# Pooling attention and a tanh-shrink MLP: four steps around batch 1 and batch 2 put in another order

## The chip, the cores and the metric

The kernel runs on one core of one Trainium2 chip. The metric is the device time of one execution in microseconds, and for several executions their median. Each time is that of a whole launch; the profile shows one execution on the same core, with a span a little shorter than the time measured around it.

## What is computed

Eight batches of eight heads, 576 positions, head size 64. Keys and values are averaged over groups of eight positions, so that each head has 72 pooled keys. Attention follows, and its output goes through an MLP whose activation is h - tanh(h).

```python
k_p = k.reshape(B, H, Sp, pool, D).mean(axis=3)
v_p = v.reshape(B, H, Sp, pool, D).mean(axis=3)
scores = scale * np.matmul(q, k_p.transpose(0, 1, 3, 2))
attn = softmax(scores)                     # over the 72 pooled keys
x = np.matmul(attn, v_p).transpose(0, 2, 1, 3).reshape(B * S, H * D)
h = x @ w_in                               # 4608 x 512 @ 512 x 2048
out = (h - np.tanh(h)) @ w_out             # @ 2048 x 512
```

## The kernel before, in words

The schedule is written out by hand. Each engine runs its instructions in the order of the text, and an instruction that waits holds up all behind it on its engine. The 4608 rows are cut in nine groups of 512. Group g < 8 is the first 512 positions of batch g; group 8 gathers the last 64 positions of all batches.

**Group 0** multiplies plainly: L588 makes h (mlp_h_mms), L599 and L601 the tanh and the difference, L616 (mlp_o) the product with w_out, in four quarters `qd` of four blocks `tb`. Between these matmuls stands the attention of batch 1: its keys are turned on TensorE (k_transpose, L352) and copied by VectorE to KB (L342, L343, L346); its q, which GpSimd's software queue has loaded as bf16 into the space of w2s[4], is reordered into q_bf (L1017, one half by VectorE, the other by ScalarE), turned on TensorE (q_pe_transpose, L228, evacuated by ScalarE at L144; q_pe_tail, L240), and used for the scores (L398). VectorE pools the values (pool_v1, L303 and L323). The product of attention and values is L487; VectorE divides it by the sum (L522, L523) into x_sb; TensorE turns x_sb (turn1, L566) and ScalarE copies it to xT (L573).

**Groups 1 to 8** use a product with seven block products in place of eight. For it, sums of blocks of w_out must be made: sum0 to sum3, `negated` and w_sum, all by w_sum at L674 (VectorE, for sum3 GpSimd) except `negated` (ScalarE, L996). They stand among the instructions of group 0 and the first pairs of group 1. Four of GpSimd's sums are released by `placed`, the last instruction of pool_v1(2, 4). In each group seven pairs of hidden tiles (h_pair, L634 on TensorE, L647 tanh on ScalarE, L648 difference on VectorE) are followed by the block products (L691); between these stand the scores (head_scores, L446, banks in pairs 2,3 then 4,5 then 0,1) and the attention output (L472) of the next batch. The banks of the pairs in group 1 are (6, 4, 2, 6, 0, 2, 4).

**q and k of batch 2 on** go through DMA transposes issued by SyncE (SP): k_dma_transpose at L374, q_dma_transpose at L214 and L219, after ScalarE's casts q_cast_part at L196 and L201. In group 1 the cast and the transpose of part p - 3 stand ahead of pair p, for p = 3, 4, 5. On SP the DMA issues are in order as well: the stores of group 0 (L707), the transpose of x (L557), the transpose of the keys of batch 2, which waits for GpSimd's pooling (L270), then the loads of batch 3. The loads of w_in and w_out (L761, L768), of v of batch 0 (L831) and q of batch 1 (L841, L842) are issued by GpSimd, behind its memsets.

PSUM banks are handed out in turn by ps_any; for batch 1 it draws on banks 4 to 7.

Of the kernel before, what the change touches and what calls it, by code (L numbers as in the profile page):

```python
# [43 lines left out]
def kernel(  # L44
# [9 lines left out]
    nc = tc.nc  # L54
# [43 lines left out]
    w2s = const.tile([128, 5, NP, HD], F16, name="w2s")  # L98
# [50 lines left out]
    def load_main(src, dst, b, t0, t1, eng=nc.sync):  # L149
        return eng.dma_start(out=dst[:, t0:t1, :], in_=src[b, 0:128, t0:t1, :])  # L150
# [12 lines left out]
    def load_k(b, eng=nc.sync):  # L163
        return [
            load_main(k_pairs, k_raw[b % 2], b, 0, NM, eng),
            load_dense(k_pairs, k_raw[b % 2], b, eng),
        ]
# [25 lines left out]
    def q_cast_part(b, n):  # L193
        t = q_raws[b]
        if n < 2:
            nc.scalar.copy(  # L196
                out=q_bf[:, 2 * n : 2 * n + 2, :, :].rearrange("p j h d -> p h j d"),
                in_=t[:, :, 2 * n : 2 * n + 2, :],
            )
        else:  # L200
            nc.scalar.copy(out=q_bf[:QT, R, :, :], in_=q_raws.pop(b)[:QT, :, R, :])  # L201
# [21 lines left out]
    def q_pe_transpose(b, hps, eng=None):  # L223
        qT, _ = q_tiles(b)
        for hp in hps:
            ps = ps_any([128, QA], FP32, "qT_ps")
            for j in range(R):
                nc.tensor.matmul(  # L228
                    ps[:, j * 128 : (j + 1) * 128],
                    lhsT=q_bf[:, j, 2 * hp : 2 * hp + 2, :].rearrange("p h d -> p (h d)"),  # L230
                    rhs=ident[:, :],
                    start=True,
                    stop=True,
                )
            evac(qT[:, :, hp, :], ps.rearrange("p (j c) -> p j c", j=R), eng)
# [64 lines left out]
    def pool_v1(ta, tb):  # L300
        r = v_raw[1].rearrange("p t (j d) -> p t j d", d=D)
        for n in (4, 2, 1):
            nc.vector.tensor_tensor(  # L303
                out=r[:, ta:tb, 0:n, :],
                in0=r[:, ta:tb, 0:n, :],
                in1=r[:, ta:tb, n : 2 * n, :],
                op=ALU.add,
            )
        if ta == NM:
            return v_left(VB[1], r[:, NM, 0:1, :], nc.vector)  # L310
        return v_main(VB[1], r[:, :, 0:1, :], nc.vector, ta, tb)
# [48 lines left out]
    def k_transpose(b, alloc, engs=(nc.vector.tensor_copy, nc.scalar.copy)):  # L360
        kd = kdups.pop(b)
        ps = alloc([128, NM, 128], FP32, "kT_ps")
        for t in range(NM):
            turn_tile(ps[:, t, :], kd, t)
        kb_main(KB[b % 2], ps, 0, NM, engs)
        ps = alloc([128, 128], FP32, "kT_ps")
        turn_tile(ps[:, :], kd, NM)
        kb_left(KB[b % 2], ps, nc.vector.tensor_copy)
# [3 lines left out]
    def k_dma_transpose(b):  # L372
        kT = work.tile([128, NT, 128], BF16, name="kT", tag="kT", bufs=1)
        nc.sync.dma_start_transpose(  # L374
            out=kT[:, :, :], in_=kdups.pop(b)[:, :, :, :].rearrange("p t a d -> p (t a d)")
        )
        kTs[b] = kT
# [232 lines left out]
    def mlp_o(g, tb, qd, gts):  # L610
        if qd == 0:
            o_tiles[tb] = bank((1, 2, 3, 0)[tb], [128, DM])
        o_ps = o_tiles[tb]
        i0 = W2_ORDER[qd]
        for i in range(i0, i0 + 4):
            nc.tensor.matmul(  # L616
                o_ps[:, :],
                lhsT=gts[i][:, tb * 128 : (tb + 1) * 128],
                rhs=w2b[:, i, :],
                start=(i == 0),  # L620
                stop=(i == NHID - 1),
            )
        if qd == 3:
            if tb < 2:
                nc.vector.tensor_copy(out=O[:, tb, :], in_=o_ps[:, :])
            else:
                nc.scalar.copy(out=O[:, tb, :], in_=o_ps[:, :])
            if tb % 2:
                store(g, tb - 1, tb + 1, nc.sync)
# [136 lines left out]
    def load_w2(i, n):  # L766
        w2_dmas.append(
            nc.gpsimd.dma_start(out=w2b[:, i : i + n, :], in_=w2_src[:, i : i + n, :])  # L768
        )
# [39 lines left out]

    make_identity(nc, ident)  # L810
    nc.gpsimd.memset(q_bf[64:128, R, :, :], 0.0)
    nc.gpsimd.memset(w2s[64:128, 3, 6:8, :], 0.0)
    nc.gpsimd.memset(mask[:, :, :], 1.0)
    for m, base, step, cm in (
        (mask[:, 0 : 2 * NM : 2, 0], G - 1, 0, -1),
# [27 lines left out]
        out=q1_bf, in_=q[1, :, 0:QA, :].rearrange("h (p j) d -> p h j d", j=R)  # L843
    )
    load_w2(8, 4)
    nc.gpsimd.memset(k_raw[1][:, NM, :], 0.0)
    nc.gpsimd.memset(v_raw[0][:, NM, :], 0.0)
    nc.gpsimd.memset(KB[1][:, :], 0.0)
# [67 lines left out]
    gts = []  # L916
# [84 lines left out]
    def sum0(k0):  # L1001
        return w_sum(w2s[:, 0, :, :], b11, b22, ALU.add, k0=k0, k1=k0 + 4)

    def sum1(k0):
        return w_sum(w2s[:, 1, :, :], b11, b12, ALU.add, k0=k0, k1=k0 + 4)
# [7 lines left out]
    pool_k(1, nc.gpsimd, last=nc.vector)  # L1013
    load_w2(4, 4)
    load_w2(12, 4)
    for h, copy in ((0, nc.vector.tensor_copy), (4, nc.scalar.copy)):
        copy(  # L1017
            out=q_bf[:, 0:R, h : h + 4, :].rearrange("p j h d -> p h j d"),
            in_=q1_bf[:, h : h + 4, :, :],
        )  # L1020
    mlp_o(0, 0, 0, gts)
    mlp_o(0, 1, 0, gts)
    mlp_o(0, 2, 0, gts)
    k_transpose(1, ps_any, (nc.vector.tensor_copy, nc.vector.tensor_copy))
    mlp_o(0, 3, 0, gts)
    q_pe_transpose(1, (0, 1), "act")
    sum1(0)
    pool_v1(0, 2)
    q_pe_transpose(1, (2, 3), "act")
    q_pe_tail(1)  # L1030
    scores_wide(1, (0,))
    placed = pool_v1(2, 4)
    mlp_o(0, 0, 1, gts)
    scores_wide(1, (1,))
    mlp_o(0, 1, 1, gts)
# [27 lines left out]
    turn1(3)  # L1063
    av(1, 4, ps_any, True)
    sum0(4)
    for tb in range(4):
        mlp_o(0, tb, 3, gts)
    x_pairs.pop((1, 0))
    x_pairs.pop((1, 1))
    x_dma_transpose(1, 2)  # L1070
    pool_k(2, nc.gpsimd)
    k_dma_transpose(2)
    load_k(3)
    pool_v(2, nc.gpsimd, (0, 1))
    k_place(2, nc.gpsimd.tensor_copy)
# [2 lines left out]
    for g in range(1, NG):  # L1078
        nb = g + 1 if g + 1 < B else None
        nn = g + 2 if g + 2 < B else None  # L1080
        for p in range(NP - 1):
            if g == 1 and 3 <= p < 6:
                q_cast_part(2, p - 3)
                q_dma_transpose(2, p - 3)
            if nb is not None and g > 1 and p < 3:
                q_cast_part(nb, p)
            h_pair(g, p, ((6, 4, 2, 6, 0, 2, 4) if g == 1 else (0, 2, 4, 6, 0, 2, 4))[p], p % 2)
            if g == 1 and p == 1:
                sum2(4)
            if g == 1 and p == 2:  # L1090
                w_sum(b12, b22, b12, ALU.subtract)
            if g == 1 and p == 5:
                load_v(3)
                load_q(3)
                v_spread(2, nc.gpsimd)
            if 3 <= p < 6:
                sum_p(2 * p - 6, 2 * p - 4)
            if g > 1 and p == 0:
                if nb is not None:
                    k_dma_transpose(nb)  # L1100
                store(g - 1, 2, 4, nc.gpsimd)
                store(g - 1, 0, 2, nc.gpsimd)
                if nb is not None:
                    k_place(nb, nc.gpsimd.tensor_copy)
            if nb is not None and g > 1 and p < 3:
                q_dma_transpose(nb, p)
            if nb is not None and g > 1 and p == 2:
                v_spread(nb)
                if nn is not None:
                    load_k(nn)  # L1110
                    load_v(nn)
                    load_q(nn)
        h_one(g, NP - 1, 1, 0, 2)
        h_one(g, NP - 1, 0, 1, 3)
        sum_p(6, 8)
        sum_q(0, 4)
        sum_q(4, 8)
        if nb is not None:
            sum_d(0, 2)
            sum_d(2, 4)  # L1120
        ps_a = Banks(2, 3, 4, 5, 0, 1)
        for u in range(14):
            n, half = u // 2, u % 2
            bk, lhs, rhs = products[n]
            if n == 6 and g == NG - 1:
                break
            product(g, bk, lhs, rhs, 4 * half, 4 * half + 4, n < 2)
            if half:
                after_product(g, n)
            if nb is not None:  # L1130
                if u == 0:
                    head_scores(nb, (0, 1))
                if u == 2:
                    head_scores(nb, (2, 3), True)
                if u in (5, 6, 7, 8, 10):
                    blk = (5, 6, 7, 8, 10).index(u)
                    av(nb, blk, ps_b1, True)
                    if blk in (1, 3, 4):
                        x_dma_transpose(nb, blk // 2)
                if u == 6 and nn is not None:  # L1140
                    pool_k(nn, nc.gpsimd)
                    pool_v(nn, nc.gpsimd)
        if g < NG - 1:
            nc.scalar.copy(out=O[:, 0:2, 0:HD], in_=chain(g, C1))  # L1144
# [37 lines left out]
```

## Time and profile before

| what | us |
|---|---|
| median of three runs | 286.86 (286.77 to 288.04) |
| the profiled execution, its own time | 286.49 |
| its span | 284.7 |
| TensorE matmul busy | 275.9 |
| VectorE busy | 224.2 |
| ScalarE busy | 155.5 |
| GpSimd busy | 119.1 |

The busy time is that of the whole span. Below, lines are shown of the chain of work that ended last (start, length, what) and of timelines (start, length, engine, line, operation, tiles and shape, count, and in brackets the idle time of the engine before it with what ended it). Several instructions of one kind in a row are merged into one line with their count. PE is TensorE, DVE VectorE, ACT ScalarE, POOL GpSimd, SP SyncE.

### The profile page before, as it was taken

The page shows a single profiled execution, that of the slowest core. Times are in us where ns is not written, and L with a number is a line of the kernel's source. Part 1 is how long each engine was busy: PE and PEld are TensorE (multiplying, and loading weights), DVE is VectorE, ACT ScalarE, POOL GpSimd, SP SyncE. Part 2 cuts the span into 40 slices and gives each one's busy share as a digit, 9 for nine tenths or more (in the row PEclk, how much of TensorE's full clock was granted, in tenths as well). Part 3 has the DMA queues.
Part 4 walks back from the last instruction along what each step waited for, and adds up shares of the span by engine and source line. Part 5 has one row for each costly group of instructions (what it writes and reads, how often), then busy time and mean ns, then how long its engine had stood idle before and what let it go on. Part 6 is the DMA issues. An engine that isn't in the chain of part 4 may idle for free.

```text
span 284.7 us, 5459 instructions
## 1 busy us (share of the span) xinstructions
PE 275.9 (97%) x2156; PEld 180.2 (63%) x2156; DVE 224.2 (79%) x339; ACT 155.5 (55%) x208; POOL 119.1 (42%) x129
## 2 busy tenths in 40 slices
PE   7899999998999999999999999999999999999994
PEld 2454455644894489448954895479547954884583
DVE  5569898789875998599859985998599839936983
ACT  2837676386628672857186718670868056216610
POOL 8810809972299019901990099009910110010000
PEclk9999999999999999999999999999999999999998
DMA  7999999889847894769789986896640540012014
GB/s 245 230 210 279 259 206 305 270 236 229 246 83 144 290 324 83 143 226 350 130 107 270 324 149 124 272 323 131 114 161 0 76 157 0 2 74 77 0 39 111
DMA packets 66731, 49.82 MB, mean 175 GB/s; under 512 B 42088, under 2 KB 55928, under 8 KB 66706
## 3 DMA queue, kind: packets, MB, share of 16 engines
q1 hardware_dynamic: 56082, 34.92, 48.8%
q0 software_dynamic: 8432, 12.72, 18.8%
q10 hardware_dynamic: 2192, 1.84, 2.2%
q8 instruction: 17, 0.28, 0.5%
q14 instruction: 8, 0.07, 0.1%
HBM read 36.70 MB, written 9.44 MB: 162 GB/s over the span
## 4 chain that ended last, share of the span: by engine, by line
PE 90%; DMA 4%; ACT 2%; issue 1%; DVE 1%; ACTq 0%
PE PS L634 36%; PE PS L691 35%; PE PS L588 5%; PE PS L616 5%; PE PS L472 3%; PE PS L446 3%; DMA qT<-q_bf 2%; DMA q_raw<-in_q_dram 2%; PE PS L398 1%; PE PS L781 1%; PE PS L487 1%; ACT q_bf L196 1%; ACT qT L144 1%; PE PS L875 0%; PE PS L936 0%
## 5 line engine op out<-in xcount | busy, mean ns | idle before, releaser
L634 PE MATMUL PS<-xT,w1b 128*128 128x512 bf16 (+1 forms) x504 | 98.0, 355 | 0.0
L648 DVE TENSOR_TENSOR Gt<-PS,TS 128x1024 bf16<-128x1024 f32 x56 | 68.4, 1222 | 33.7 <-ACT TS L647 33.7
L634 PEld LDWEIGHTS <-w1b 128*128 128x128 f16 x576 | 56.3, 98 | 52.8
L647 ACT ACTIVATE TS<-PS 128x1024 f32<-128x1024 f32 x56 | 57.4, 1025 | 29.5 <-PE PS L634 27.4
L735 POOL TENSOR_TENSOR m<-O,m 128x512 f32<-128x512 f32 x6 | 7.6, 1259 | 77.3 <-ACT m L733 77.3
L691 PE MATMUL PS<-w2s,Dg 128*128 128x256 f16 x256 | 30.2, 273 | 0.0
L467 ACT ACTIVATE E<-PS 72x1024 bf16<-72x1024 f32 (+1 forms) x30 | 26.1, 930 | 4.8 <-PE PS L446 4.6
L691 PEld LDWEIGHTS <-Gt 128*128 128x128 bf16 x256 | 23.6, 98 | 6.9 <-issue 2.5
L261 POOL TENSOR_TENSOR k_raw<-k_raw 128x512 f32<-128x512 f32 (+2 forms) x13 | 21.1, 1636 | 14.6 <-DMA k_raw<-in_k_dram 14.6
L691 PEld LDWEIGHTS <-P 128*128 128x128 bf16 x256 | 24.6, 98 | 3.0
L691 PEld LDWEIGHTS <-Dg 128*128 128x128 bf16 x256 | 24.6, 98 | 2.8
L656 DVE TENSOR_TENSOR P<-Gt 128x1024 bf16<-128x1024 bf16 x32 | 22.0, 687 | 0.5
L707 POOL DMA_DIRECT2D out_dram<-O x14 | 7.7, 551 | 31.7 <-DVE O L745 29.5
L742 ACT COPY m<-PS 128x512 f32<-128x512 f32 x8 | 4.7, 586 | 29.6 <-PE PS L691 29.6
L666 DVE TENSOR_TENSOR Dg<-Gt 128x1024 bf16<-128x1024 bf16 x32 | 20.4, 683 | 0.0
L523 DVE TENSOR_TENSOR x_sb<-PS,rden 128x512 bf16<-128x512 f32 x28 | 19.4, 692 | 1.0
L282 POOL TENSOR_TENSOR v_raw<-v_raw 128x512 f32<-128x512 f32 (+1 forms) x12 | 18.2, 1537 | 0.0
L691 PE MATMUL PS<-w2s,Gt 128*128 128x256 f16 x128 | 16.4, 273 | 0.0
L691 PE MATMUL PS<-w2b,P 128*128 128x256 f16 x128 | 16.3, 273 | 0.0
L691 PE MATMUL PS<-w2s,Q 128*128 128x256 f16 x128 | 16.3, 272 | 0.0
L691 PE MATMUL PS<-w2b,Gt 128*128 128x256 f16 x128 | 16.3, 272 | 0.0
L1144 ACT COPY O<-PS 128x512 f32<-128x512 f32 x7 | 4.1, 587 | 21.9 <-PE PS L691 21.9
(125 smaller groups left out, 403.9 us busy)
## 6 DMA issues: line engine op xcount, KB each, us to landing
k_raw<-in_k_dram SPq DMA_DIRECT2D x7, 1024.0 KB, 5.9
out_dram<-O POOLq DMA_DIRECT2D x14, 512.0 KB, 4.3
v_raw<-in_v_dram SPq DMA_DIRECT2D x6, 1024.0 KB, 8.0
q_raw<-in_q_dram SPq DMA_DIRECT2D x6, 1024.0 KB, 10.6
w1b<-in_moe_w_in_dram POOLq DMA_DIRECT2D x4, 512.0 KB, 13.3
w2b<-in_moe_w_out_dram POOLq DMA_DIRECT2D x4, 512.0 KB, 16.6
v_raw<-in_v_dram SPq DMA_DIRECT2D x2, 512.0 KB, 12.5
out_dram<-O SPq DMA_DIRECT2D x2, 512.0 KB, 3.5
```

The costliest lines, as they stand in the source:

```text
L261: eng.tensor_tensor(out=r[:, ta:tb, 0:4, :], in0=r[:, ta:tb, 0:4, :], in1=r[:, ta:tb, 4:8, :], op=ALU.add,)
L282: eng.tensor_tensor(out=r[:, ta:tb, 0:4, :], in0=r[:, ta:tb, 0:4, :], in1=r[:, ta:tb, 4:8, :], op=ALU.add,)
L467: nc.scalar.activation(out=e, in_=ps, func=ACT.Exp, scale=SCALE)
L523: nc.vector.tensor_tensor(out=x_sb[:, :, :, :], in0=ps[:, :, :, 0:D], in1=rden[:, :, :, :].to_broadcast([128, 2, 4, D]), op=ALU.mult,)
L588: nc.tensor.matmul(h_tiles[i][:, :], lhsT=w1b[:, fb, i * 128 : (i + 1) * 128], rhs=xT[g][:, :, fb, :], start=(fb == 0), stop=(fb == NFB - 1),)
L616: nc.tensor.matmul(o_ps[:, :], lhsT=gts[i][:, tb * 128 : (tb + 1) * 128], rhs=w2b[:, i, :], start=(i == 0), stop=(i == NHID - 1),)
L634: nc.tensor.matmul(dst[:, t0 * 128 : t1 * 128], lhsT=w1b[:, fb, i * 128 : (i + 1) * 128], rhs=x[:, t0:t1, fb, :], start=(fb == 0), stop=(f ...
L647: nc.scalar.activation(out=t2, in_=PS[:, b0 : b0 + 2, :], func=ACT.Tanh)
L648: nc.vector.tensor_sub(out=Gt[:, p, :, :], in0=PS[:, b0 : b0 + 2, :], in1=t2)
L656: nc.vector.tensor_tensor(out=P[:, a:b, :], in0=Gt[:, a:b, 0, :], in1=Gt[:, a:b, 1, :], op=ALU.add)
L666: return nc.vector.tensor_tensor(out=Dg[:, a:b, :, :], in0=Gt[:, a:b, :, 0:HT], in1=Gt[:, a:b, :, HT:TG], op=ALU.subtract,)
L691: nc.tensor.matmul(part(g, bk, tt), lhsT=lhs(k, slice(tt * 128, (tt + 1) * 128)), rhs=rhs[:, k, :], start=(first and k == 0 and (tt == 0 o ...
```

## The change

1. A memset of the last rows of q's tail of batch 1 (GpSimd, L812) moves from ahead of the mask and the first loads to a place behind the load of the third quarter of w_out.
2. The second half of the reordering of q of batch 1 goes from ScalarE to VectorE; the first two pairs of q's turns on TensorE go ahead of mlp_o(0, 3, 0); sum1(0) goes behind pool_v1(2, 4).
3. The stores of group 0, which mlp_o(0, tb, 3) issues, go behind the transposes of x's last rows and of the keys of batch 2 on SP.
4. In group 1 the casts and transposes of q of batch 2 stand one pair sooner, and with them the loads of v and q of batch 3 and the spread of v.

```diff
     make_identity(nc, ident)
     nc.gpsimd.memset(q_bf[64:128, R, :, :], 0.0)
-    nc.gpsimd.memset(w2s[64:128, 3, 6:8, :], 0.0)
     nc.gpsimd.memset(mask[:, :, :], 1.0)
...
     load_w2(8, 4)
+    nc.gpsimd.memset(w2s[64:128, 3, 6:8, :], 0.0)
     nc.gpsimd.memset(k_raw[1][:, NM, :], 0.0)
...
-    for h, copy in ((0, nc.vector.tensor_copy), (4, nc.scalar.copy)):
-        copy(
+    for h in (0, 4):
+        nc.vector.tensor_copy(
             out=q_bf[:, 0:R, h : h + 4, :].rearrange("p j h d -> p h j d"),
             in_=q1_bf[:, h : h + 4, :, :],
         )
...
     k_transpose(1, ps_any, (nc.vector.tensor_copy, nc.vector.tensor_copy))
+    q_pe_transpose(1, (0, 1), "act")
     mlp_o(0, 3, 0, gts)
-    q_pe_transpose(1, (0, 1), "act")
-    sum1(0)
     pool_v1(0, 2)
     q_pe_transpose(1, (2, 3), "act")
     q_pe_tail(1)
     scores_wide(1, (0,))
     placed = pool_v1(2, 4)
+    sum1(0)
     mlp_o(0, 0, 1, gts)
...
-    for tb in range(4):
-        mlp_o(0, tb, 3, gts)
     x_pairs.pop((1, 0))
     x_pairs.pop((1, 1))
     x_dma_transpose(1, 2)
     pool_k(2, nc.gpsimd)
     k_dma_transpose(2)
+    for tb in range(4):
+        mlp_o(0, tb, 3, gts)
     load_k(3)
...
-            if g == 1 and 3 <= p < 6:
-                q_cast_part(2, p - 3)
-                q_dma_transpose(2, p - 3)
+            if g == 1 and 2 <= p < 5:
+                q_cast_part(2, p - 2)
+                q_dma_transpose(2, p - 2)
...
-            if g == 1 and p == 5:
+            if g == 1 and p == 4:
                 load_v(3)
                 load_q(3)
                 v_spread(2, nc.gpsimd)
```

## The prediction

> **What bounds the kernel now.** I read the page first, then the chain of work that ended last, then the timelines of the engines around the edited lines.
>
> ```profile
> PE 275.9 (97%) x2156; PEld 180.2 (63%) x2156; DVE 224.2 (79%) x339; ACT 155.5 (55%) x208; POOL 119.1 (42%) x129
> ```
>
> TensorE is busy 97% of the span, and the chain is 90% PE. The change removes no matmul, so only the holes in PE's stream can be won. From 20 us on, the busy time by stage has three stretches with holes: 0.21 us between 30 and 40 us, 0.15 between 40 and 50, 0.85 between 60 and 70. Every other stretch up to 270 us is full. The chain shows two of the three places.
>
> ```profile
> 37.21 0.86 PE PS L616 x4
> 38.07 0.24 PE PS L228 x4
> 38.31 0.02 issue
> 38.33 0.25 ACT qT L144
> 38.58 0.21 issue
> 38.82 0.60 ACT qT L144
> 39.42 0.04 issue
> 39.46 0.38 PE PS L398
> ...
> 63.51 6.34 DMA qT<-q_bf
> 69.84 0.14 issue
> 69.98 0.62 PE PS L446 x4
> ```
>
> At 38 us PE turns q of batch 1 and waits for ScalarE to empty the banks (L144). Near 70 us it waits for the second DMA transpose of q of batch 2, which started when its ScalarE cast ended at 63.48.
>
> The next lines are the VectorE timeline, then the GpSimd timeline (start, duration, engine, line).
>
> ```profile
> 43.13 1.64 DVE L674 TENSOR_TENSOR w2s<-w2b 128x1024 f16<-128x1024 f16 x1
> 45.21 0.69 DVE L523 TENSOR_TENSOR x_sb<-PS,rden 128x512 bf16<-128x512 f32 x1
> 81.06 1.93 DVE L743 TENSOR_TENSOR m<-m,m 128x512 f32<-128x512 f32 x1 [0.46 <-ACT m L742]
> ```
>
> ```profile
> 42.70 1.53 POOL L674 TENSOR_TENSOR w2s<-w2b 128x512 f16<-128x512 f16 x1 [7.24 <-DVE VB L323]
> 44.19 1.59 POOL L674 TENSOR_TENSOR w2s<-w2b 128x512 f16<-128x512 f16 x1
> 80.91 1.54 POOL L267 TENSOR_TENSOR k_raw<-k_raw 128x640 f32<-128x640 f32 x1
> ```
>
> A weight sum on VectorE costs 0.69 us alone (sum1(0) at 38.22), but the one at 43.13 took 1.64 and ended at 44.77, which is 0.58 after GpSimd's operation ended at 44.19. L743 shows the same: shortest 0.69, here 1.93, ended 0.54 after GpSimd's add at 82.45. So a VectorE add with two SBUF inputs that finds GpSimd in an operation waits for its end, then runs some 0.58 more. GpSimd waits in turn: its 1.53 and 1.59 are 1.15 in the two of that group that met no VectorE sum.
>
> **What the Trainium skill says.** "SBUF — State Buffer", section "Who interferes with whom": a VectorE instruction with two SBUF inputs and a GpSimd instruction that reads SBUF share one port; the second to issue blocks wholly until the first is done. The trace agrees (1.64 against 0.69, 1.93 against 0.69). "DMA: Bandwidth & Descriptors", section "Issuing engines are not separate DMA queues": transfers of all issuers run on the same 16 DMA engines and interleave. The trace agrees for the loads after 9 us; before 8.4 us the software queue has no packet at all, though its first issue began at 4.36.
>
> **Part A, the memset.** It occupies GpSimd from 1.91 to 2.43; without it the software-queue issues that follow (v at 4.36, w1 from 5.92, w2 at 8.86) come about 0.5 us sooner. The later ones (q of batch 1 at 11.13, w2 at 12.78) sit behind a cast that waits until 10.58 for another load, so they do not move. At its new place it delays three memsets by 0.5; GpSimd is idle there for 14.37 us until 29.47, and the dense k load that needs one of them is issued at 18.87. Packets of the software queue now begin between 8.4 and 8.6; 0.5 sooner they meet only the tail of the first loads, since the q piece on the chain had landed at 7.30 and the k piece by 8.13. Upper bound: half the engines taken for 0.5 us, +0.25. Lower bound: the queue, full until q of batch 1 lands at 36.5, drains sooner, but VectorE is busy with kd until 36.44, so its q copy at 36.60 gains at most 0.13. I take 0.
>
> **Part B, q of batch 1.** ScalarE's copy cost 1.05 (36.60 to 37.65), VectorE's 0.43. With both on VectorE, q is complete at about 37.40. PE now turns the first two head pairs directly after the keys at 37.21, which need only the first half (ready 37.03), and the 0.86 us of L616 lie behind them while ScalarE empties the banks. Before, PE took 39.46 - 37.21 = 2.25 for this piece; its work is 0.86 + 16 turns at 0.055 (0.88) + 0.12 for the tail = 1.86. Gain 0.39: the scores start at 39.07. I find no new wait in it: the banks of the other two pairs are emptied by VectorE's key copies at about 38.4, and PE comes at 38.51.
>
> VectorE: the key copies start at about 37.38 instead of 37.19 (+0.19); sum1(0) is gone from here (-0.61, from its start to the next one's). So pool_v1 ends, and `placed` falls, at 42.61 + 0.19 - 0.61 = 42.19; call it X. GpSimd's four subtractions are released by `placed`, at X + 0.09. Three sums, not two, now stand there ahead of the reciprocals that PE needs. First: X - 0.09 to X + 0.59, it has the port first, as before. GpSimd's first is held and ends at X + 1.62 (44.23 before). Second: held, ends X + 2.16 (44.77 before). GpSimd's second has been waiting and takes the port, as its first did before; it ends at X + 3.17 (45.78 before). Third: held until then, ends X + 3.75. Reciprocal and x_sb end at X + 4.65 = 46.84. Before, x_sb ended at 45.90 and PE's turn of it (L566) started at 46.07, with nothing to spare. Now PE arrives at 46.07 - 0.39 = 45.68 and gets x_sb at 46.84 + 0.06 = 46.90: a hole of 1.2 us. Queued behind on PE are turn1(0), turn1(1) and the rest of group 0; behind it every span to 54.4 us is PE or a wait on PE's own results, so nothing absorbs it. Part B: 46.90 - 46.07 = +0.8. Bounds: -0.39 if the sums ran at 0.69 (ending by X + 2.0 = 44.2, before PE's av); -0.2 if only one sum were held; +0.95 if the key copies come 0.15 later too.
>
> **Part C, keys ahead of stores and q one pair sooner.** On SP the stores now stand behind the key transpose, which waits for kd (GpSimd, 55.17). They issue at about 56.4 instead of 54.99; O is next written after 73 us, so nobody waits. The k load of batch 3 follows at 58.0 instead of 59.47. The v and q loads of batch 3 go a pair sooner with the transposes, and GpSimd's spread of v is bound by its own chain until 63.8. Casts: after the second tanh (57.94) ScalarE takes the cast at 58.86 and the third tanh at 59.80 instead of 59.66; so +0.14 once, and the gaps of 0.70 and the removed later casts take up the rest. The casts end at 59.90 and 61.77 instead of 61.62 and 63.48. With the old 6.34 us the second transpose lands at 61.8 + 6.34 = 68.1, before PE comes at 69.13. In this frame the k load is over 1.4 us ahead too, so I expect no longer time.
>
> What is late next is VectorE. `head_scores` writes banks 2,3, then 4,5; banks 4,5 are read by pair 6's subtraction (L648, 68.33 + 1.22 = 69.55), and VectorE has no idle time from 60.1 to 69.5. The third tanh pushes it by about 0.13: 69.68. PE's second pair of score matmuls starts at 69.73, ends at 70.04; before, they ended at 70.60. Gain 0.56, not 0.85. Ends: -0.85 if that bank is not waited for, 0 if the transpose is no sooner.
>
> **Sum.** 0 + 0.8 - 0.56 = +0.24. The profiled execution took 286.49 (span 284.7, 1.79 around it), so it becomes 286.7; the median of the three runs shown is 286.86, 0.37 higher, so 287.1.
>
> **Rivals.**
> 1. The sums are held once or not at all (GpSimd's second subtraction loses the port, or starts later). For: which of two waiters wins is read from one place only. Against: there and at L743 VectorE always waited. Part B is then -0.39 to -0.2, and with -0.56 the sum is about -0.85: 286.0. Chance 0.2.
> 2. Slower: the q transposes still end last. The place is PE's first score matmuls in group 1; the price is the 0.56 of part C; it decides from the point at which the second transpose takes over 7.9 us from its cast (61.8 to 69.7) in place of 6.34, as it may, since stores and k load now stand directly ahead. For: in later groups the transposes took a median 3.4, here 5.5 to 6.3 beside loads. Against: the loads are sooner as well. +0.8 alone: 287.7, up to 288.3 if it lands 0.6 later than now. Chance 0.15.
> 3. The q edit does not do what it says: q of batch 1 lands too late for the turn at 37.21 (slack 0.18). PE would only shift by that delay, which lies in the hole of 1.2 us: no change in the sum. It is inside the forecast.
>
> **How the numbers follow.** Forecast 287.1 (286.7 to 287.5), chance 0.6; rivals 0.2 and 0.15; 0.05 for the rest. Half of rival 1 and most of rival 2 are needed for 8 in 10: 286.1 to 287.9. About 0.5% (1.43 us) is what a measurement of this kernel can tell from no change. Faster than 285.43 needs both best ends (-0.39 - 0.85 and a bit of A): 0.08. Slower than 288.29 needs both bad ends: 0.07. Same: 0.85.
>
> **What would show it.** B: L398 of batch 1 near 39.1; three L674 on VectorE after L323, the last ending near 46; a PE hole of about 1.2 us before the first L566. C: no PE wait on the qT transpose; casts L196 one pair sooner; a wait of some 0.3 us between the L446 pairs on VectorE's L648. A: the first L588 still near 19.0. The prediction is wrong if x_sb is ready by 45.7, or if PE still waits for qT.

## The result and the profile after

The changed kernel takes 288.05 us (median of 20 executions, 286.77 to 291.29), the kernel before 286.44 beside it (20 executions). The ratio is 1.0064, interval 1.0036 to 1.0091: slower by 0.64%, 1.6 us between the medians. The forecast was 287.1 with a range of 286.1 to 287.9; the time lies 0.15 us above that range. Medians here and below are of all executions, and a ratio leaves out those that took over 1.5% more than the fastest of the same kernel (one of the changed kernel, four of run e5). Six of the 20 executions took 290 us or more, with a mean granted TensorE clock of 0.992 to 0.997; the profiled one took 287.07 (span 285.3) at 1.000, so it shows a milder case than the median.

The page's first part, for the kernel after:

```profile
PE 276.0 (97%) x2155; PEld 179.8 (63%) x2156; DVE 224.3 (79%) x340; ACT 154.5 (54%) x207; POOL 118.4 (42%) x129
```

The work is the same as before to 0.1 us on TensorE, so what was lost is holes, stretches in which TensorE stands idle. The chain that ended last, after:

```profile
36.48 0.76 DVE q_bf L1017 x2
37.24 0.36 DVE KB L342
...
41.97 2.78 DVE w2s L674 x3
44.75 0.97 issue
45.96 0.70 DVE x_sb L523
46.71 0.40 PE PS L566 x4
...
62.58 7.75 DMA qT<-q_bf
70.46 0.69 PE PS L446 x4
```

The two places are still those of the chain before, but their content is new. At 38 us ScalarE's evacuation is gone from the chain; in its place stands VectorE, from the q copies to the three weight sums and x_sb. Near 70 us the q transpose is still there, and it takes 7.75 us in place of 6.34. TensorE's timeline, after, with the idle time ahead of each group in brackets:

```profile
39.49 1.02 PE L616 MATMUL PS<-w2b,Gt 128*128 128x512 f16 x4 [0.27 <-DMA w2b<-in_moe_w_out_dram]
46.71 0.40 PE L566 MATMUL PS<-ident,x_sb 128*128 128x128 bf16 x4 [0.82 <-DVE x_sb L523]
70.46 0.69 PE L446 MATMUL PS<-qT,KB 64*72 64x512 bf16 x4 [0.55 <-DMA qT<-q_bf]
```

One hole was forecast (46.71), one is new and small (39.49: the product of the second quarter now comes before its weights have landed), and one was forecast to go and stayed (70.46), though shorter than the 0.85 us of before. In this execution the scores start 0.48 us later than before (69.98); 0.75 us of delay were there when group 1 began (first L634 at 55.01, before at 54.26), so the second place still gained 0.27. The median lies 1.0 us above this execution; where the executions without a trace lose that is not shown here, and e2 and e4 below show what it can be.

The three sums of the forecast, on VectorE and then on GpSimd, after:

```profile
41.88 0.68 DVE L674 TENSOR_TENSOR w2s<-w2b 128x1024 f16<-128x1024 f16 x1
42.48 1.64 DVE L674 TENSOR_TENSOR w2s<-w2b 128x1024 f16<-128x1024 f16 x1
44.05 1.64 DVE L674 TENSOR_TENSOR w2s<-w2b 128x1024 f16<-128x1024 f16 x1
45.96 0.69 DVE L523 TENSOR_TENSOR x_sb<-PS,rden 128x512 bf16<-128x512 f32 x1
```

```profile
42.05 1.52 POOL L674 TENSOR_TENSOR w2s<-w2b 128x512 f16<-128x512 f16 x1 [6.38 <-DVE VB L323]
43.55 1.59 POOL L674 TENSOR_TENSOR w2s<-w2b 128x512 f16<-128x512 f16 x1
45.10 1.59 POOL L674 TENSOR_TENSOR w2s<-w2b 128x512 f16<-128x512 f16 x1
```

The two engines take turns at the port that they share: the sum of 42.48 ends at 44.12, 0.55 after GpSimd's first operation (43.57), that of 44.05 at 45.69, 0.55 after its second (45.14).

### The profile page after: what moved, and what is told of

It reads as the page before. It is cut to its first block, busy times and chain, and to the rows that moved or that the text cites. A ratio compares the mean times of both kernels' runs of the same rounds, so it can differ in the third digit from the quotient of the medians.

```text
span 285.3 us, 5461 instructions
## 1 busy us (share of the span) xinstructions
PE 276.0 (97%) x2155; PEld 179.8 (63%) x2156; DVE 224.3 (79%) x340; ACT 154.5 (54%) x207; POOL 118.4 (42%) x129
## 4 chain that ended last, share of the span: by engine, by line
PE 78%; DMA 14%; DVE 4%; ACT 1%; issue 1%; POOL 0%; ACTq 0%; POOLq 0%
PE PS L634 35%; PE PS L691 34%; DMA w2s<-in_q_dram 9%; PE PS L472 3%; DMA qT<-q_bf 3%; PE PS L446 3%; DMA v_raw<-in_v_dram 3%; PE PS L616 2%; DVE v_raw L303 1%; DVE w2s L674 1%; ACT q_bf L196 1%; PE PS L566 0%; ACT TS L647 0%; DVE VB L323 0%; DVE q_bf L1017 0%
## 5 line engine op out<-in xcount | busy, mean ns | idle before, releaser
L634 PE MATMUL PS<-xT,w1b 128*128 128x512 bf16 (+1 forms) x504 | 98.0, 355 | 0.0
L634 PEld LDWEIGHTS <-w1b 128*128 128x128 f16 x576 | 56.3, 98 | 52.9
L691 PE MATMUL PS<-w2s,Dg 128*128 128x256 f16 x256 | 30.2, 272 | 0.0
L691 PEld LDWEIGHTS <-Gt 128*128 128x128 bf16 x256 | 23.5, 98 | 6.8 <-issue 2.3
L691 PEld LDWEIGHTS <-P 128*128 128x128 bf16 x256 | 24.6, 98 | 3.0
L691 PEld LDWEIGHTS <-Dg 128*128 128x128 bf16 x256 | 24.7, 98 | 2.8
L691 PE MATMUL PS<-w2s,Gt 128*128 128x256 f16 x128 | 16.4, 273 | 0.0
L691 PE MATMUL PS<-w2b,P 128*128 128x256 f16 x128 | 16.3, 273 | 0.0
L691 PE MATMUL PS<-w2b,Gt 128*128 128x256 f16 x128 | 16.3, 272 | 0.0
L691 PE MATMUL PS<-w2s,Q 128*128 128x256 f16 x128 | 16.3, 272 | 0.0
```

The lines of the kernel that those rows point to most:

```text
L634: nc.tensor.matmul(dst[:, t0 * 128 : t1 * 128], lhsT=w1b[:, fb, i * 128 : (i + 1) * 128], rhs=x[:, t0:t1, fb, :], start=(fb == 0), stop=(f ...
L691: nc.tensor.matmul(part(g, bk, tt), lhsT=lhs(k, slice(tt * 128, (tt + 1) * 128)), rhs=rhs[:, k, :], start=(first and k == 0 and (tt == 0 o ...
```

## The experiments

All ratios are to the kernel before on the same chip, with 95% intervals. Four theories are tested. Theory 1: three weight sums in a row are held by GpSimd, and x_sb is late. Theory 2: the loss comes from the order on SP and the q transposes of batch 2. These two were stated after the result; the next two, which divide theory 2, after the first four runs. Theory 3: SP stands at the key transpose, stores and k load start later, and the q transposes land behind their bytes. Theory 4: it is their own earlier start that makes the q transposes slow.

| run | edit | us | ratio |
|---|---|---|---|
| the change | all four parts | 288.05 | 1.0064 [1.0036, 1.0091] |
| e1 | q part of batch 1 alone | 286.94 | 1.0036 [1.0023, 1.0050] |
| e2 | SP order and q of batch 2 sooner | 288.74 | 1.0108 [1.0079, 1.0137] |
| e3 | memset alone | 286.18 | 1.0002 [0.9991, 1.0012] |
| e4 | the change, sum1(0) put back | 289.58 | 1.0133 [1.0117, 1.0149] |
| e5 | SP order alone | 287.75 | 1.0046 [1.0026, 1.0065] |
| e6 | q of batch 2 sooner alone | 286.35 | 1.0008 [0.9993, 1.0023] |
| e7 | the change, stores first, sum1(0) later | 286.45 | 1.0007 [0.9996, 1.0019] |
| e8 | the change, stores first | 287.07 | 1.0036 [1.0024, 1.0048] |
| e9 | the change, stores issued by ScalarE | 287.47 | 1.0039 [1.0020, 1.0058] |
| e10 | the change, k load behind q transposes | 286.87 | 1.0021 [1.0014, 1.0029] |
| e11 | version made from the findings | 285.53 | 0.9978 [0.9966, 0.9990] |
| e12 | e4 with zero matmuls in the hole | 288.58 | 1.0074 [1.0049, 1.0098] |

**e1, the q part alone** (in the kernel before: point 2 of the change).

> The kernel before with only the reordering of q of batch 1 on VectorE, the earlier turn of its first pairs and sum1(0) behind pool_v1(2, 4). Theory 1 (three sums back to back are held by GpSimd, x_sb is late): slower by 0.7 to 1.0 us, with TensorE idle about 1 us before the first L566. Theory 2 (the loss comes from the order on SP and the q transposes of batch 2): no change or faster by up to 0.4 us.

Measured: +0.8 us between the medians (286.94 to 286.13), as theory 1 had it. TensorE stood idle 0.95 us before the first L566, at 46.70. In that execution TensorE also waited 0.80 us for the first q copy, because it was early and q of batch 1 lands at about 36.5 whatever TensorE does.

**e2, SP order and q of batch 2 together.**

> The kernel before with only the SP order (key transpose ahead of the stores) and the q of batch 2 one pair sooner. Theory 1: faster by 0.2 to 0.6 us. Theory 2 (transposes that start sooner beside the k load take longer and land no sooner, in some executions later than before): between no change and slower by 1 us, with a longer time to landing than the 5.5 and 6.3 us of before.

Measured: slower by 1.1%, 2.6 us between the medians, more than the whole change. Theory 1 alone is out: the larger loss is in the part that was forecast as a gain. TensorE waited 1.64 us for qT, with 7.2 and 7.8 us to landing.

**e3, the memset alone.**

> The kernel before with only the memset moved. Both theories: within 0.3 us of before. A third (software-queue loads that start 0.5 us sooner slow the first loads): slower by 0.3 to 1 us, with the second q cast (L866) later than before.

Measured: no change. The third possibility named there (not theory 3) falls.

**e4, sum1(0) put back.**

```diff
+    sum1(0)
     pool_v1(0, 2)
...
     placed = pool_v1(2, 4)
-    sum1(0)
```

> The changed kernel with sum1(0) put back ahead of pool_v1(0, 2). Theory 1: two sums, not three, stand ahead of the reciprocal; x_sb ends near where it did before (0.2 later), the hole before L566 shrinks to about 0.4 us, and the kernel is 0.6 to 0.8 us faster than the changed one, near the kernel before. Theory 2: no faster than the changed one by over 0.2 us.

Measured: the hole before L566 went away wholly (45.88, no wait), and the kernel became 1.5 us slower than the changed one. No theory had that. What was won at 46 us was paid back with more on top at 70, as the windows and TensorE's timeline of e4 show (in the first fence the columns are the window, then busy time and count of each engine, the granted clock, the DMA share and GB/s):

```profile
60.00:70.00 10.00, 9.10 (x46) 4.30 (x44) 9.93 (x12) 7.19 (x9) 4.12 (x8) 1.00 1.07 204
70.00:80.00 10.00, 8.33 (x71) 6.04 (x72) 6.51 (x12) 5.52 (x7) 0.13 (x1) 0.83 0.81 234
```

```profile
68.07 1.04 PE L691 MATMUL PS<-w2s,Gt 128*128 128x256 f16 x8
71.67 1.06 PE L446 MATMUL PS<-qT,KB 64*72 64x512 bf16 x4 [2.56 <-DMA qT<-q_bf]
72.67 1.89 PE L691 MATMUL PS<-w2s,Gt 128*128 128x256 f16 x8
```

TensorE comes 0.8 us sooner than in the profiled execution of the change, and the second transpose lands 1.2 us later (71.5 against 70.3), though it was issued sooner (62.00 against 62.58); together that makes a hole of 2.56 us. After it the granted clock was 0.50 from 72 to 75 us (0.83 over the window of ten), and eight L691 matmuls that took 1.04 us ahead of it took 1.89.

**e5 and e6, the two halves of e2 apart.**

> The kernel before with only the key transpose ahead of the stores on SP; q of batch 2 stays where it was. Theory 3 (SP stands at the key transpose until kd is ready, the stores and the k load of batch 3 start 1.5 to 3 us later, and the q transposes land behind their bytes): slower by 1.5 to 3 us, q transposes landing at 70.5 us or later. Theory 4 (it is the earlier start of the q transposes that makes them slow): within 0.3 us of before.

> The kernel before with only the q of batch 2 one pair sooner; the stores stay ahead of the key transpose. Theory 3: the q transposes land before 69 us, TensorE waits 0 to 0.4 us for VectorE's subtraction of pair 6 instead, faster by 0 to 0.6 us. Theory 4: slower by 1 us or more, time to landing 7 us or more.

Measured: e5 slower by 0.46%; 1.5 us between the medians (287.75 to 286.26), the lower end of the forecast, and between 285.58 and 290.82 from execution to execution; in its profile the transpose landed at 70.5 and TensorE waited 1.94 us. Theory 4 is out as the cause of the loss. But e6 gained nothing either: its transposes, cast and issued a pair sooner, took 6.8 and 7.7 us to landing, and TensorE's line of e6 is

```profile
70.45 0.62 PE L446 MATMUL PS<-qT,KB 64*72 64x512 bf16 x4 [1.12 <-DMA qT<-q_bf]
```

So moving the issue forward moves the landing little: the transposes wait for something else. The DMA view tells what. For the kernel before, the microseconds from 62, 64 and 66 (packets, bytes, rate, then packets by size):

```profile
DMA packets 168, 0.34 MB, mean 344 GB/s; under 512 B 0, under 2 KB 0, under 8 KB 168
DMA packets 345, 0.37 MB, mean 374 GB/s; under 512 B 182, under 2 KB 182, under 8 KB 345
DMA packets 1020, 0.25 MB, mean 253 GB/s; under 512 B 1020, under 2 KB 1020, under 8 KB 1020
```

For e2, the microseconds from 64, 66 and 68:

```profile
DMA packets 149, 0.31 MB, mean 305 GB/s; under 512 B 0, under 2 KB 0, under 8 KB 149
DMA packets 438, 0.36 MB, mean 357 GB/s; under 512 B 298, under 2 KB 298, under 8 KB 438
DMA packets 1152, 0.29 MB, mean 287 GB/s; under 512 B 1152, under 2 KB 1152, under 8 KB 1152
```

In these windows packets of 2 KB and more are the k load of batch 3, packets under 512 B the transposes. In both kernels the transposes move almost nothing until the k load is through, and then they follow at once: at 64 before, at 66 in e2. They stand behind the k load in SP's queue, as that stands behind the stores. "DMA: Bandwidth & Descriptors", section "Queues, rings and completion order", of the Trainium skill says that descriptors of one issuing engine's queue are consumed in ring order on each DMA engine; these lines agree. SP's own issues show it too. Of the two q transposes the second has the longer issue (shortest, median and longest in ns):

```profile
L214 SPq DMA_TRANSPOSE qT<-q_bf x2: 1269/1963/2657, 61.6 to 63.5; - x2
L214 SPq DMA_TRANSPOSE qT<-q_bf x2: 1437/2660/3884, 60.7 to 62.6; - x2
L214 SPq DMA_TRANSPOSE qT<-q_bf x2: 2064/3033/4002, 61.7 to 63.8; - x2
L214 SPq DMA_TRANSPOSE qT<-q_bf x2: 1231/1232/1232, 60.3 to 62.2; - x2
```

These are before, after, e2, and e10, a later run whose k load is behind the transposes. And the stores are late because SP stands at the key transpose. SP's issues, before and then after:

```profile
54.99 1.60 SPq L707 DMA_DIRECT2D out_dram<-O  x2
56.65 1.46 SPq L557 DMA_TRANSPOSE xT_last<-x_end  x1
58.20 1.22 SPq L374 DMA_TRANSPOSE kT<-kd  x1
59.47 0.58 SPq L150 DMA_DIRECT2D k_raw<-in_k_dram  x1
```

```profile
54.73 1.81 SPq L374 DMA_TRANSPOSE kT<-kd  x1
56.63 1.01 SPq L707 DMA_DIRECT2D out_dram<-O  x2
57.69 0.84 SPq L150 DMA_DIRECT2D k_raw<-in_k_dram  x1
```

In e2, where kd was later still (SP issued the key transpose at 57.03), the DMA engines ran empty meanwhile; the window of e2 and that of the kernel before, share and GB/s last:

```profile
56.00:58.00 2.00, 2.00 (x14) 1.21 (x13) 0.16 (x1) 1.02 (x1) 2.00 (x2) 1.00 0.09 19
```

```profile
56.00:58.00 2.00, 2.00 (x12) 0.92 (x10) 0.73 (x1) 1.09 (x2) 2.00 (x2) 1.00 1.03 406
```

Two microseconds in which 406 GB/s flowed before, mostly stores, and 19 now: that is the delay that the q transposes meet later. Their second issue ends at 66.2 before and at 67.8 in e2, and they land 3.7 and 3.8 us after that, at 69.8 and 71.6.

How late kd is differs between the profiles: 54.7 in the change, 55.2 before, 55.6 in e5, 57.0 in e2. In e2 GpSimd waited 1.48 us for the k load of batch 2, in e5 1.00, before 0.24, in the change not at all. No edit moves that load, so part of the spread between executions may come from it; that was not tested.

In the profiled execution of the change the queue explains less. The second issue ends at 66.5, 0.3 us later than before, and the landing is 0.5 later. In e4 it ends at 66.2, as before, and the landing is 1.7 us later than before. There the packets of SP's queue fell from 572 in the half microsecond from 66.5 to 257 in the next and stayed low, and in the change from 399 to 200, while packets of GpSimd's spread of v were moving; in the kernel before these came from 67.25, when the transposes were nearly through. No run moves the spread of v alone, so whether it slows the transposes is open.

**e7 and e8, the stores back in front.**

```diff
+    for tb in range(4):
+        mlp_o(0, tb, 3, gts)
     x_pairs.pop((1, 0))
...
     k_dma_transpose(2)
-    for tb in range(4):
-        mlp_o(0, tb, 3, gts)
```

e7 also has sum1(0) behind that loop, in place of behind pool_v1(2, 4).

> The changed kernel with the stores back ahead of the key transpose and sum1(0) behind the last quarter of group 0, after VectorE's copies of O. Theory 3 with theory 1: no hole before the first L566 (two sums stand ahead), no wait on the q transposes: faster than before by 0.4 to 1.0 us. If sum1(0) in its new place delays group 1's first subtraction, no change.

> The changed kernel with only the stores back ahead of the key transpose. Theory 3: the loss of the q part stays (0.7 to 1.0 us), the wait on the q transposes goes: 0.3 to 0.7 us slower than before. Theory 4: as slow as the changed kernel or slower.

Measured: e8 has no wait on qT and the loss of the q part (1.0036, as e1), as theory 3 has it; its interval overlaps that of the change. e7 missed: it has neither the hole at L566 nor a wait for qT, and is no faster than before. TensorE's lines of e7 show holes of another kind:

```profile
62.79 3.61 PE L634 MATMUL PS<-xT,w1b 128*128 128x512 bf16 x16 [0.28 <-DVE Gt L648]
66.79 1.89 PE L634 MATMUL PS<-xT,w1b 128*128 128x512 bf16 x8 [0.39 <-DVE Gt L648]
70.39 0.41 PE L446 MATMUL PS<-qT,KB 64*72 64x512 bf16 x2 [0.50 <-DVE Gt L648]
```

VectorE is late in group 1. Two things push it in the trace: it waits for ScalarE's tanh, which now stands behind the earlier casts, and sum2(4) at 59.62 took 1.99 us beside GpSimd. The three holes, 0.28, 0.39 and 0.50 us, sum to 1.17, in place of the one of 0.85 before. Neither push was tested alone.

**e9 and e10, the wait taken away in two other ways.** e9 issues the two stores from ScalarE's queue behind its copies of O; e10 puts the k load behind the q transposes:

```diff
     k_dma_transpose(2)
     for tb in range(4):
         mlp_o(0, tb, 3, gts)
-    load_k(3)
...
             if g == 1 and p == 4:
+                load_k(3)
                 load_v(3)
```

> The changed kernel with the two stores of group 0 issued by ScalarE behind its own copies of O, so that they don't stand behind the key transpose on SP; the order on SP is otherwise that of the change. Theory 3 (the delayed stores and k load are what the q transposes wait for): the stores move before 57 us, the q transposes land 1 to 2 us sooner, and the kernel is 0.6 to 1.5 us faster than the changed one, at the loss of the q part alone (0.7 to 1.0 us slower than before). If the key transpose's place itself is what slows the q transposes: as slow as the changed kernel.

> The changed kernel with the k load of batch 3 behind the q transposes of batch 2 (with the v load). Theory 3, second half (the transposes stand behind the 1.1 MB of the k load): time to landing of the q transposes falls from about 8 to 3 to 5 us, the wait of TensorE on them goes, leaving the loss of the q part: 0.7 to 1.0 us slower than before. If they are slow for another reason: no faster than the changed kernel.

Measured: both took the wait on qT away with the keys still first on SP, so the place of the key transpose is not itself the trouble; taking either the stores or the k load from ahead of the q transposes is enough. (e9's interval overlaps that of the change, e10's does not.) e9's transposes took 5.7 and 6.7 us (1.0039, the loss of the q part again). e10 has the stores no sooner than the change (57.26 against 56.63), yet transposes issued at 60.34 and 62.20 had moved nearly all their packets by 66, and the loss fell to 0.21%, from 0.64%. Its profile gives no time to landing for them, since nothing waited. In both, TensorE's second pair of L446 waits for VectorE in its place, 0.25 us in e9 and 0.50 in e10.

**e11, a version faster than both kernels.** Point 1 and the q turn of the change; sum1(0) and sum2(4) behind the last quarter of group 0; the subtraction from b12 in two halves; stores first; q of batch 2 at its old pairs; the k load behind the q transposes. The cut is against the kernel before.

```diff
     for tb in range(4):
         mlp_o(0, tb, 3, gts)
+    sum1(0)
+    sum2(4)
...
-            if g == 1 and p == 1:
-                sum2(4)
-            if g == 1 and p == 2:
-                w_sum(b12, b22, b12, ALU.subtract)
+            if g == 1 and p in (1, 2):
+                w_sum(b12, b22, b12, ALU.subtract, k0=4 * p - 4, k1=4 * p)
...
             if g == 1 and p == 5:
+                load_k(3)
                 load_v(3)
```

> Version made from the findings: memset and q part of the change, sum1(0) and sum2(4) behind the last quarter of group 0, w_sum of b12 in halves at pairs 1 and 2, stores ahead of the key transpose, q of batch 2 at its old pairs, k load of batch 3 behind the q transposes. Gains expected 0.4 us at the q turn and 0.6 to 0.85 us near 70 us: faster than before by 0.8 to 1.3 us. If VectorE's sums at the end of group 0 are held by GpSimd for long: 0 to 0.5 us.

Measured: 285.53, faster than before by 0.22% (0.10 to 0.34), 0.64 us between the medians; less than the 0.8 expected. Both places run without a wait:

```profile
45.54 0.40 PE L566 MATMUL PS<-ident,x_sb 128*128 128x128 bf16 x4
68.64 0.81 PE L446 MATMUL PS<-qT,KB 64*72 64x512 bf16 x4
```

**e12, the clock.** e4 with ten matmuls of zeros into a free bank, between the first block product of group 1 and the scores.

> The changed kernel with sum1(0) put back, plus ten matmuls of zeros between the first block product of group 1 and the first scores, in the place where TensorE stood idle for 2.56 us. If the loss there beyond the hole itself is a lower granted clock after the hole: 1 to 2 us faster than the same kernel without them (289.58), with full granted clock between 70 and 80 us. If not: the same or slower.

Measured: 288.58 against 289.58 for e4, intervals apart (1.0049 to 1.0098, 1.0117 to 1.0149). The window that stood at a granted clock of 0.83 in e4:

```profile
70.00:80.00 10.00, 8.92 (x85) 6.30 (x84) 7.49 (x13) 5.40 (x7) 0.37 (x1) 1.00 0.93 248
```

TensorE still waited 1.03 us for qT after them in this execution, the slowest of the six (289.45). The edit saves no work, so the 1 us that came back between the medians is put down to the clock. "TensorE: Matmul & The Clock Gate", section "HAM oscillation — how this bites in real kernels", of the Trainium skill warns of idle gaps beyond about 3.4 us; here 2.56 us was enough, and the measurement decides.

## Why the prediction was wrong

**Part A was right.** Taken as 0; e3 gives 1.0002.

**Part B was right in mechanism, place and size.** Forecast +0.8; e1 gives +0.8. The alternation of the port between VectorE and GpSimd came as worked out, each held sum at 1.64 us. The hole was forecast at 1.2 us and was 0.82, for two reasons: x_sb ended 0.19 us sooner than forecast (46.65 in place of 46.84), and TensorE came 0.21 later (45.89 in place of 45.68), having waited 0.15 us for the q copy and 0.27 for weights landing at 39.5, where the forecast said "I find no new wait in it".

**Part C was wrong, and with it the sum.** Forecast -0.56; e2 gives +2.6. The prediction's own sign of being wrong, "if PE still waits for qT", came: 0.55 us in the changed kernel's trace. The step that failed is "With the old 6.34 us the second transpose lands at 61.8 + 6.34 = 68.1". It took a time to landing for a property of the transfer. It was mostly time in the queue behind the k load: issued sooner, the transposes of e6 took 7.7 us and landed at 70.3, against 69.8 in the kernel before. The gain of issuing sooner was nothing (1.0008). Nor is 6.34 fixed at the old place: in e3, which has the order of before there, the k load was through by 64 us and the transposes took 4.1 and 4.3. The second failed step is of the stores: "O is next written after 73 us, so nobody waits". Nobody waits for the stores, but k load and q transposes stand behind their 1 MB in the same queue, so a wait of SP for kd can reach TensorE: 1.7 us of it in e2, 0.3 us in the profiled execution of the change. The argument that the k load is issued sooner (57.69, forecast 58.0) did not help, since its bytes stand behind those of the stores. What else made the transposes late in the change and in e4 is open, as said above.

**The bank after the transpose was right as a place.** The forecast was a wait of 0.3 us on pair 6's subtraction once qT is no longer late; with no wait on qT it was 0.50 in e7, e8 and e10 and 0.25 in e9, and none in e11.

**The slower rival was the right one, and was given 0.15.** Rival 2 named the place (first scores of group 1), the reason (stores and k load directly ahead) and a decision point, 7.9 us from the cast to landing. The changed kernel's profiled execution stayed just under it (7.8, cast to 62.54, landing at 70.33); e4 and e2 went beyond, with 9.5 and 7.8 from the issue, which in e2 came 1.5 us after the cast. Its range of 287.7 to 288.3 holds the measured 288.05, in part by luck: it allowed 0.6 us beyond the lost gain, and e2 alone loses 2.6. Its price also had no term for the clock: in e4 the hole is followed by matmuls at little over half speed.

**The parts don't add.** e1, e2 and e3 sum to 1.0036 + 1.0108 + 1.0002 - 2 = 1.0146; the change is 1.0064. The q part makes TensorE late by 0.75 us at group 1, and that much of the wait for qT is then covered. e4 agrees: with the hole of the q part repaired the kernel loses more. The halves of part C don't add either: e5 and e6 sum to 1.0054, e2 is 1.0108. What makes up the rest in both sums was not tested. That the executions of 290 us and more of the changed kernel, at a clock of 0.992 to 0.997, are those whose hole was long enough fits e4 (0.992) but was not shown, since only one execution has a trace.

## What to carry to other kernels

A time from issue to landing includes, as here, what stands ahead in the same queue: look at which packets move when before crediting an earlier issue, and count the bytes ahead of a transfer rather than its issue time. An instruction that waits on an issuing queue delays whatever is behind it, and the one who pays may be two transfers further on. When two losses lie on one engine's path, repairing the first alone can make the second larger; test repairs together as well as apart.

## What was not expected of the hardware

A hole of 2.56 us on TensorE cost more than its length: the granted clock in the following window was 0.83 and a group of eight matmuls took 1.89 us in place of 1.04; holes of 1.64 (e2), 1.94 (e5) and 0.82 us (the change) showed no lower clock in the windows after them. Whether the length alone decides, and from where on, these runs do not show. VectorE and GpSimd, three sums each side by side, took the shared port in turn: the first VectorE sum took 0.68 us, the second and third 1.64 each.
